# All of TensorE's products as pairs in its two row halves, with four equal PSUM tiles and written-out engine orders

## The chip, the core and the metric

The kernel runs on one core of a Trainium2 chip. The metric is device time in microseconds (us) of one execution. A core has five engines with instruction streams of their own: TensorE (PE in the profile, its weight loads PEld), VectorE (DVE), ScalarE (ACT), GpSimd (POOL) and SyncE (SP), which here issues DMAs. TensorE writes to PSUM, eight banks of 512 fp32 columns on 128 partitions.

## What is computed

Block-sparse attention over 4 batches, 8 heads, 768 tokens and 64 channels a head, followed by a feed-forward layer with a squared ReLU:

```python
scores = (q @ k.T) / 8                # per batch and head, 768 x 768
scores = where(mask, scores, -1e9)    # window, first and last block, 3 random blocks of 32
attn = exp(scores - max) / sum(...)
x = (attn @ v)                        # joined over heads: 3072 x 512
out = relu(x @ w_in)**2 @ w_out       # w_in 512 x 2048, w_out 2048 x 512
```

Inputs and output are fp32; the kernel multiplies in bf16.

## The kernel before

Heads are worked two at a time, as 16 units `u` (4 batches of 4 pairs). A head has 64 channels, so q and k of two heads fill the 128 partitions.

**Scores (L456, with L460 for a mask added as a product).** For 256 queries (128 at the start of batch 0) and two key blocks of 128, four matmuls with 64 rows each write one two-bank tile X: head 0 in TensorE's upper row half and bank 0, head 1 in the lower half and bank 1. ACT takes the exponential of the 1024 columns (L467) to the bf16 tile pT, DVE multiplies by the 0/1 mask MK (L474).

**Values (L496).** 128-row matmuls of 65 columns (64 channels and a column of ones for the sum) gather pT times V over six key blocks in the one-bank tile po. DVE normalizes (L504, L506) to xq; x is then transposed into xT, by TensorE in batch 0 (L513), by DMA later (L525).

**Feed-forward.** `hidden` (L554) multiplies w_in with xT into an X tile, for a unit of 768 columns (two blocks of 128 hidden rows for 384 queries) in batches 1 to 3, or 512 in batch 0, with 128 rows, four matmuls deep. `relu` goes to ACT (L563) or DVE (L565), `square` to POOL (L575) or ACT (L573), giving g. `output` (L598) sums 16 matmuls of 512 columns in the one-bank tile py for each 128 queries; it is copied to ys (L250 ACT, L252 DVE) and stored by SP (L607). For the last queries the output is cut into 512, 256, 128 and 128 columns, in py and X tiles by turns.

**PSUM.** X tiles of two banks (two at first, beside two single banks F for transposes and masks, later a third in the place of these), one bank po, one bank py.

**Order.** All instructions are tasks with assumed lengths. `run_schedule` walks through them at build time and picks what starts first, with keys, a pacing of the scores and small pseudo-random ties (`SEEDS`); the program is emitted in that order, so each engine's order is fixed at build. Scores are emitted in groups of one to three tiles (`GROUPS`), because a change between 64-row and 128-row matmuls has a price (`SWITCH`) there.

Of the kernel before, what the change touches and what calls it, by code (L numbers as in the profile page):

```python
# [19 lines left out]
P = 128  # L20
# [5 lines left out]
def kernel(  # L26
# [27 lines left out]
    TWM = 768  # L54
# [5 lines left out]
    PT_BUFS, R_BUFS, G_BUFS, XT_BUFS = 6, 4, 34, 3  # L60
# [4 lines left out]
    ps_o = ctx.enter_context(tc.psum_pool(name="ps_o", bufs=1))  # L65
    ps_y = ctx.enter_context(tc.psum_pool(name="ps_y", bufs=1))
# [8 lines left out]
    CB, GATES = 0.4, (6, 7)  # L75
    GROUPS = (1, 2, 2), (2, 2, 2), (2, 2, 3), (3, 3, 3)
    QT0, ADDED, ALONE = [(0, 128), (128, 128), (256, 256), (512, 256)], (0, 128), (0, 128)
# [4 lines left out]
    SWITCH, SHARE, SLACK = 0.096, 0.85, 0.1  # L82
    AHEAD = {"PE": 0.008, "DVE": 0.131, "ACT": 0.168, "POOL": 0.0, "SP": 0.0}
    LEAD = 6.401
    HOLD = 0
    PACE0, PACE, SINGLE, MASK_AT = 38.799, 1.711, 1, 17.0

    class Buf:
        def __init__(self, pool):
# [5 lines left out]
    TIES = 2.554, 0.816  # L99
    SEEDS = (  # L100
            512149, 706682, 47083, 521312, 863273, 189227, 137643, 472468, 522007,
            987534, 137643, 876738, 345072, 137643, 631945, 518011, 946966, 257531,
            137643, 137643, 206493, 528378, 381761, 582778)

    def tie(n):
        x = (n + 1) * 2654435761 & 0xFFFFFFFF ^ SEEDS[n // 64] * 2246822519 & 0xFFFFFFFF
        x = (x ^ x >> 15) * 2246822519 & 0xFFFFFFFF
        return (x ^ x >> 13) / 4294967296.0 - 0.5

    class Task:  # L110
        def __init__(self, engs, key, fn, deps=(), get=(), put=(), after=0.0, mode=None, dma=0.0, late=None, bias={}, port=False,
                     lead=0.0, yields=False, paced=False):
            self.engs = engs if isinstance(engs, dict) else dict([engs])
            self.key, self.fn = key, fn
            self.deps, self.get, self.put = list(deps), list(get), list(put)
            self.after, self.mode, self.dma, self.late, self.bias = after, mode, dma, late, bias
            self.port, self.lead, self.yields, self.paced = port, lead, yields, paced
            self.end = self.eng = None
            self.order = len(tasks)
            self.key += TIES[0 if key < 300 else 1] * tie(self.order)  # L120
            for b in self.put:
                b.holds += 1
            tasks.append(self)

    def run_schedule(free, bufs, dma_free, mode=128):
        taken = {name: [] for name in bufs}
        cells = [None] * 6
        paced = [t for t in tasks if t.paced]
        port = {"DVE": (0.0, 0.0), "POOL": (0.0, 0.0)}
        last = {"DVE": None, "POOL": None}  # L130
        waiting = list(tasks)
        ready = []
# [5 lines left out]
        singles = sum(b.pool == "X1" for t in tasks for b in t.get)  # L138

        def bank(pool, now):  # L140
            n, best = (1, None) if pool == "X1" else (2, None)
            for c in (4, 5) if pool == "X1" else (0, 2) if singles else (0, 2, 4):
                mine = [cells[i] for i in range(c, c + n)]
                if c in gone or any(b and b.holds for b in mine):
                    continue
                r = max([now] + [b.free for b in mine if b])
                k_ = (round(max([now] + [b.free + 0.8 for b in mine if b]), 4), c)
                if best is None or k_ < best[0]:
                    best = (k_, c, r)
            return best  # L150

        relaxed, gone = False, set()
        while waiting or ready:
            while paced and paced[0].end is not None:
                paced.pop(0)
            due = 1e9
            if paced and all(d.end is not None for d in paced[0].deps):
                due = max([paced[0].after] + [seen(d, "PE") for d in paced[0].deps])
            now = [t for t in waiting if all(d.end is not None for d in t.deps)]
            if now:  # L160
                gone = set(map(id, now))
                waiting = [t for t in waiting if id(t) not in gone]
                ready += now
            found, urgent = [], {}
            spare = sum(not any(b and b.holds for b in cells[c:c + 2]) for c in ((0, 2) if singles else (0, 2, 4)))
            for t in ready:
                r0 = t.after
                ok = True
                cnt, spot = {}, {}
                gone.clear()  # L170
                for b in t.get:
                    if b.pool in ("X1", "X2"):
                        x = bank(b.pool, free["PE"])
                        if x is None:
                            ok = False
                            break
                        gone.add(x[1])
                        spot[id(b)] = x[1]
                        r0 = max(r0, x[2])
                        continue  # L180
                    held = taken[b.pool]
                    at = len(held) + cnt.get(b.pool, 0) - bufs[b.pool]
                    cnt[b.pool] = cnt.get(b.pool, 0) + 1
                    if at >= 0:
                        if held[at].holds:
                            ok = False
                            break
                        r0 = max(r0, held[at].free)
                if not ok:
                    continue  # L190
                opt = None
                for e, us in t.engs.items():
                    r = max([r0, free[e]] + [seen(d, e) - t.lead for d in t.deps])
                    sw = SWITCH if e == "PE" and t.mode and t.mode != mode else 0.0
                    if e == "POOL" or (e == "DVE" and t.port):
                        p0, p1 = port["DVE" if e == "POOL" else "POOL"]
                        us += SHARE * max(0.0, min(r + us, p1) - max(r, p0))
                    if opt is None or r + us + t.bias.get(e, 0.0) < opt[3] - 1e-9:
                        opt = (r + us + sw, r, e, r + us + t.bias.get(e, 0.0))
                if t.yields and not relaxed and due - HOLD < opt[1] and spare <= len(paced[0].get):  # L200
                    continue
                found.append((round(opt[1], 4), t.key, t.order, t, opt, spot))
                if t.key < 100:
                    urgent[opt[2]] = min(urgent.get(opt[2], 1e9), opt[1])

            best = min((c for c in found if c[1] < 100 or c[0] + AHEAD[c[4][2]] < urgent.get(c[4][2], 1e9)),
                       key=lambda c: c[:3], default=None)
            if best is None and not relaxed:
                relaxed = True
                continue  # L210
            relaxed = False
            assert best is not None, "no task can start"
            t, (end, at, e, _) = best[3], best[4]
            t.eng = e
            t.end, free[e] = end, end - OVER[e]
            if e == "POOL" or (e == "DVE" and t.port):
                port[e] = (at, end)
                o = "DVE" if e == "POOL" else "POOL"
                more = SHARE * max(0.0, min(end, port[o][1]) - max(at, port[o][0]))
                if more and last[o]:  # L220
                    last[o].end += more
                    for b in last[o].put:
                        b.free = max(b.free, last[o].end + LAT[o])
                    free[o] += more
                    port[o] = (port[o][0], port[o][1] + more)
                last[e] = t
            if e == "PE" and t.mode:
                mode = t.mode
# [3 lines left out]
            for b in t.get:  # L232
                if b.pool in ("X1", "X2"):
                    b.at = best[5][id(b)]
                    cells[b.at] = b
                    singles -= b.pool == "X1"
                    if b.pool == "X2":
                        cells[b.at + 1] = b
# [5 lines left out]
            ready.remove(t)  # L244
            t.fn(e)
        return max(free.values())
# [54 lines left out]
    bm = consts.tile([nb, P], BF, name="bm")  # L301
# [4 lines left out]
    X = [ps_x.tile([P, 1024], F32, name=f"X{i}") for i in range(2)]  # L306
    first_pool = tc.psum_pool(name="ps_f", bufs=1)
    ps_f = first_pool.__enter__()
    FB = [ps_f.tile([P, 512], F32, name=f"F{i}") for i in range(2)]
# [527 lines left out]
```

## Time and profile before

| | |
|---|---|
| time, median of 3 runs | 271.95 us (270.59 to 272.35) |
| profiled execution, span | 270.3 us |
| TensorE busy | 260.7 us (96%), clock 1.0 from start to end |
| ACT / DVE / POOL busy | 220.8 / 174.4 / 93.4 us |
| matmul records, by row count | 2285 with 128 rows, 720 with 64, 2 with 24 (the program has 3048 matmuls) |
| HBM read, written | 27.3 MB, 6.3 MB |

A line of the groups reads: line, engine, operation, tiles, shapes, count, then busy us and mean ns of one, then the idle time just before and what ended it. "64*128" is a matmul in one row half; "128*128" takes the whole array. A TensorE row is longer than the matmul's share of the stream, because matmuls overlap in the array; the step from one start to the next is what a matmul costs in a run.

### The profile page before, as it was taken

How to read it: one execution, taken by the hardware profiler on the slowest of the kernel's cores; microseconds unless marked ns; L12 is line 12 of the kernel's file. 1: busy time of each engine (PE TensorE's matmuls, PEld its weight loads, DVE VectorE, ACT ScalarE, POOL GpSimd, SP SyncE). 2: the span in 40 equal slices, each digit the busy share in tenths (PEclk: the TensorE clock that was granted, in tenths of full speed). 3: DMA queues.
4: the chain of work that ended last, by engine and by line, in shares of the span. 5: the costliest groups of instructions: out<-in, count | busy, mean ns of one | idle time of the engine just before them, and what ended most of it. 6: DMA issues, size and time to landing. Idle time of an engine off the chain costs nothing.

```text
span 270.3 us, 7348 instructions
## 1 busy us (share of the span) xinstructions
PE 260.7 (96%) x3007; PEld 165.1 (61%) x3048; DVE 174.4 (65%) x337; ACT 220.8 (82%) x293; POOL 93.4 (35%) x114
## 2 busy tenths in 40 slices
PE   8999999999999999999999999999999999999993
PEld 5768866686665656555555555655665656555553
DVE  6788879988797999846886666777656654110100
ACT  3888999978999998999998789999989898455510
POOL 3290554746522045643343123122131123332300
PEclk9999999999999999999999999999999999999999
DMA  6999999999931238349951141336311102011022
GB/s 189 370 261 207 201 206 345 325 292 325 281 120 51 68 69 249 48 77 266 264 188 37 43 106 52 79 82 98 59 51 49 47 25 61 1 40 52 27 78 80
DMA packets 52026, 36.93 MB, mean 137 GB/s; under 512 B 31000, under 2 KB 49048, under 8 KB 51992
## 3 DMA queue, kind: packets, MB, share of 16 engines
q1 hardware_dynamic: 47224, 31.86, 43.2%
q0 software_dynamic: 4224, 4.19, 9.5%
q8 instruction: 24, 0.39, 0.6%
q10 hardware_dynamic: 544, 0.39, 0.5%
q14 instruction: 10, 0.08, 0.1%
HBM read 27.26 MB, written 6.29 MB: 124 GB/s over the span
## 4 chain that ended last, share of the span: by engine, by line
PE 85%; DMA 7%; DVE 5%; issue 2%; SPq 1%; ACT 1%; DVEq 0%; ACTq 0%
PE X L554 28%; PE py L598 26%; PE po L496 13%; PE X L456 13%; DVE pT L474 3%; DMA qs<-in_q_dram 3%; PE F L554 3%; DMA ks<-in_k_dram 2%; DMA out_dram<-ys 2%; PE X L598 1%; DVE xq L506 1%; PE F L378 1%; SPq L278 0%; PE F L408 0%; PE po L513 0%
## 5 line engine op out<-in xcount | busy, mean ns | idle before, releaser
L467 ACT ACTIVATE pT<-X 128x1024 bf16<-128x1024 f32 (+1 forms) x148 | 138.6, 1004 | 8.3 <-PE X L456 5.5
L474 DVE TENSOR_TENSOR pT<-pT,MK 128x1024 bf16<-128x1024 bf16 x132 | 103.0, 805 | 18.5 <-ACT pT L467 18.0
L575 POOL TENSOR_TENSOR g<-r 128x384 bf16<-128x384 f32 (+1 forms) x68 | 65.0, 961 | 130.2 <-ACT r L563 107.7
L598 PE MATMUL py<-w_out_sb,g 128*128 128x512 bf16 (+2 forms) x343 | 88.9, 367 | 3.0 <-issue 1.6
L554 PE MATMUL X<-xT,w_in_sb 128*128 128x384 bf16 (+1 forms) x512 | 90.8, 312 | 0.1
L554 PEld LDWEIGHTS <-w_in_sb 128*128 128x128 bf16 x640 | 54.4, 98 | 27.9 <-issue 1.0
L496 PEld LDWEIGHTS <-pT 128*128 128x128 bf16 x1152 | 47.3, 98 | 20.1 <-issue 6.2
L563 ACT ACTIVATE r<-X 128x768 f32<-128x768 f32 (+1 forms) x56 | 42.9, 766 | 19.0 <-PE X L554 17.4
L496 PE MATMUL po<-VT,pT 128*128 128x65 bf16 x1152 | 54.3, 194 | 0.6 <-DVE xq L506 0.2
L598 PEld LDWEIGHTS <-g 128*128 128x128 bf16 x416 | 34.7, 97 | 27.0 <-issue 3.8
L456 PE MATMUL X<-QK 64*128 64x256 bf16 (+1 forms) x624 | 46.1, 263 | 0.2
L456 PEld LDWEIGHTS <-QK 64*128 64x128 bf16 x624 | 25.4, 94 | 20.0 <-issue 16.1
L573 ACT ACTIVATE g<-r 128x384 bf16<-128x384 f32 (+1 forms) x52 | 27.9, 539 | 4.4 <-DVE r L565 3.0
L252 DVE COPY ys<-py 128x512 f32<-128x512 f32 (+1 forms) x14 | 9.2, 658 | 30.5 <-PE py L598 28.7
L252 POOL CAST VT<-vs 128x768 bf16<-128x768 f32 x15 | 15.4, 1024 | 30.1 <-issue 14.2
L504 DVE RECIPROCAL rs<-po 128x4 f32<-128x4 f32 (+1 forms) x52 | 9.2, 177 | 25.2 <-PE po L496 24.9
L506 DVE TENSOR_TENSOR xq<-po,rs 128x256 bf16<-128x256 f32 (+1 forms) x52 | 21.0, 404 | 1.8
L252 DVE CAST qc<-qs 128x768 bf16<-128x768 f32 (+2 forms) x16 | 9.1, 571 | 2.3 <-DMA qs<-in_q_dram 2.3
L250 ACT COPY ys<-py 128x512 f32<-128x512 f32 (+1 forms) x10 | 5.7, 571 | 5.5 <-PE py L598 5.3
L252 DVE CAST qc<-ks 128x768 bf16<-128x768 f32 (+1 forms) x13 | 9.8, 759 | 0.1
L565 DVE TENSOR_SCALAR r<-X 128x512 f32<-128x512 f32 (+1 forms) x8 | 6.6, 824 | 3.3 <-PE X L554 2.7
L554 PE MATMUL F<-xT,w_in_sb 128*128 128x128 bf16 x128 | 8.3, 219 | 0.0
(59 smaller groups left out, 90.4 us busy)
## 6 DMA issues: line engine op xcount, KB each, us to landing
vs<-in_v_dram SPq DMA_DIRECT2D x16, 384.0 KB, 6.2
out_dram<-ys SPq DMA_DIRECT2D x23, 256.0 KB, 2.2
ks<-in_k_dram SPq DMA_DIRECT2D x15, 384.0 KB, 5.3
qs<-in_q_dram SPq DMA_DIRECT2D x12, 384.0 KB, 4.8
w_in_sb<-in_moe_w_in_dram POOLq DMA_DIRECT2D x4, 512.0 KB, 9.5
w_out_sb<-in_moe_w_out_dram POOLq DMA_DIRECT2D x4, 512.0 KB, 16.3
qs<-in_q_dram SPq DMA_DIRECT2D x4, 256.0 KB, 8.2
xT<-xq SPq DMA_TRANSPOSE x36, 2.3
```

The source lines that it names most:

```text
L252: (V if e == "DVE" else G).tensor_copy(out=out, in_=in_)
L456: nc.tensor.matmul(ps[:, h, j * w:(j + 1) * w], QK[i][hs, 1, ksl], QK[i][hs, 0, qsl], start=j == 0, stop=not add, skip_group_check=True)
L467: A.activation(out=pT[:, :, 0:n], in_=stile.pop(a)[:, :, 0:n], func=AF.Exp, scale=scale)
L474: V.tensor_tensor(out=pT, in0=pT, in1=m[:, None].broadcast_to([P, 2, len(cs), w]), op=AOP.mult)
L496: nc.tensor.matmul(po[:, qc, h, :], pT[:, h, j * w + qc * P:j * w + (qc + 1) * P], VT[i][:, h, n, 0:VW], start=(n == 0 and qc == 0 and h = ...
L504: V.reciprocal(out=rs, in_=po[:, :, :, D:VW])
L506: V.tensor_tensor(out=xq, in0=po[:, :, :, 0:D], in1=rs.broadcast_to([P, n, 2, D]), op=AOP.mult)
L554: nc.tensor.matmul(htile[T, f][:, i], w_in_sb[:, kc, (f + i) * P:(f + i + 1) * P], xT[b][:, kc, c0:c0 + w], start=(kc == 0), stop=(kc == K ...
L563: A.activation(out=to, in_=src, func=AF.Relu)
L573: A.activation(out=g, in_=r, func=AF.Square)
L575: (G if e == "POOL" else V).tensor_mul(out=g, in0=r, in1=r)
L598: nc.tensor.matmul(ytile[T, i], gtile[T, f][:, ts * P:(ts + 1) * P], w_out_sb[:, f, cs[0]:cs[1]], start=(f == 0), stop=(f == NF - 1))
```

## The change

Every product is now made of 64-row matmuls, issued in pairs by `pair`: one in the upper half, one in the lower, into the two banks of one tile. Where the contraction has 128 rows (values, hidden, output), the work goes over its list twice: in the first pass half 0 writes bank 0 and half 1 bank 1, in the second pass ("crossed") half 0 adds to bank 1 and half 1 to bank 0. The two banks hold different results: two heads, two sets of hidden rows, two blocks of 128 queries or two ranges of columns. Between the passes `change_places` makes TensorE wait for the last matmul of the first pass, by a semaphore of its own; in the built program this wait stands on the next weight load.

PSUM is four two-bank tiles X for everything. Hidden units have 1024 columns; all tiles of batches 1 to 3 have 256 queries; an output accumulation covers 256 queries (two banks of 512). Values start only when all three pT tiles of their queries are there. Scores are no longer grouped. Buffers: 8 pT (6 before), 3 r (4), 13 g of 1024 columns (34 of 512). `run_schedule` with its keys, pacing and ties is replaced by `run_orders`, which takes each engine's task order from a list in the file (`ORDERS`), and so also fixes which of ACT, DVE and POOL does a task. The matmul count goes from 3048 to 5932.

```diff
+    HALVES = slice(0, D), slice(D, P)
+    def pair(out, lhsT, rhs, crossed=False, **kw):
+        for r, rows in enumerate(HALVES):
+            last = nc.tensor.matmul(out(r ^ crossed), lhsT(r ^ crossed, rows), rhs(r ^ crossed, rows), skip_group_check=True, **kw)
+        return last.ins
+
+    def change_places(last):
+        tc.add_manual_dep(nc.tensor.nop().ins, last.name, SYNC, reason="the other row half writes the bank next")
...
     def values(...):
-                    nc.tensor.matmul(po[:, qc, h, :], pT[:, h, j * w + qc * P:j * w + (qc + 1) * P], VT[i][:, h, n, 0:VW],
-                                     start=(n == 0 and qc == 0 and h == 0), stop=n == NCH - 1,
-                                     skip_group_check=True)
+                    last = pair(lambda h: po[:, h, qc], lambda h, rows: pT[rows, h, j * w + qc * P:j * w + (qc + 1) * P],
+                                lambda h, rows: VT[i][rows, h, n, 0:VW], crossed, start=not crossed and n == 0 and qc == 0,
+                                stop=crossed and n == NCH - 1)
...
     def hidden(T, f, part, parts, buf, e):
-            nc.tensor.matmul(htile[T, f][:, i], w_in_sb[:, kc, (f + i) * P:(f + i + 1) * P], xT[b][:, kc, c0:c0 + w],
-                             start=(kc == 0), stop=(kc == KM - 1))
+        crossed = part >= parts // 2
+        if part == parts // 2:
+            change_places(hlast.pop((T, f)))
+        work_ = [(j, kc) for j in range(n) for kc in range(KM)]
+        k_ = len(work_) * 2 // parts
+        for j, kc in work_[part % (parts // 2) * k_:(part % (parts // 2) + 1) * k_]:
+            hlast[T, f] = pair(lambda i: htile[T, f][:, i, j * w:(j + 1) * w],
+                               lambda i, rows: w_in_sb[rows, kc, (f + i * n + j) * P:(f + i * n + j + 1) * P],
+                               lambda i, rows: xT[b][rows, kc, c0:c0 + w], crossed,
+                               start=not crossed and kc == 0 and j == 0, stop=crossed and kc == KM - 1)
...
     def output(...):
-            nc.tensor.matmul(ytile[T, i], gtile[T, f][:, ts * P:(ts + 1) * P], w_out_sb[:, f, cs[0]:cs[1]],
-                             start=(f == 0), stop=(f == NF - 1))
+            ylast[T, i] = pair(lambda c: ytile[T, i][:, c], lambda c, rows: gtile[T, f][rows, tokens(c)],
+                               lambda c, rows: w_out_sb[rows, f, columns(c)], crossed,
+                               start=not crossed and f == 0, stop=crossed and f == NF - 1)
...
-    run_schedule({"PE": 4.4, "DVE": 4.4, "ACT": 3.65, "POOL": 3.7, "SP": 16.0},
-                 {"po": 1, "y": 1, "pT": PT_BUFS, "r": R_BUFS, "g": G_BUFS, "ys": YS_BUFS,
+    run_orders(ORDERS, {"PE": 4.4, "DVE": 4.4, "ACT": 3.65, "POOL": 3.7, "SP": 16.0},
+                 {"y": 1, "S": 2, "H": 2, "po": 2, "pT": PT_BUFS, "r": R_BUFS, "g": G_BUFS, "ys": YS_BUFS,
```

The transposes by TensorE and the mask products are turned into pairs in the same way, and 14 idle matmuls that keep TensorE busy in the opening stay.

## The prediction

> **What bounds the kernel now.** I read the busy shares and the chain first, then the groups, then TensorE's timeline at single groups.
>
> ```profile
> PE 260.7 (96%) x3007; PEld 165.1 (61%) x3048; DVE 174.4 (65%) x337; ACT 220.8 (82%) x293; POOL 93.4 (35%) x114
> PEclk9999999999999999999999999999999999999999
> PE 85%; DMA 7%; DVE 5%; issue 2%; SPq 1%; ACT 1%; DVEq 0%; ACTq 0%
> ```
>
> TensorE is busy for 96% of the span at full clock and is 85% of the chain; DMA is on the chain only in the opening (until 16.6 us) and in the last store. So the question is what TensorE's time consists of. A matmul's row is longer than its share of the stream, so I use the distance from start to start.
>
> ```profile
> 240.65 1.14 PE L554 MATMUL X<-xT,w_in_sb 128*128 128x384 bf16 x6
> 241.63 0.59 PE L598 MATMUL py<-w_out_sb,g 128*128 128x512 bf16 x2
> 242.06 1.14 PE L554 MATMUL X<-xT,w_in_sb 128*128 128x384 bf16 x6
> ...
> 149.63 1.46 PE L598 MATMUL py<-w_out_sb,g 128*128 128x512 bf16 x6
> 151.02 0.83 PE L456 MATMUL X<-QK 64*128 64x256 bf16 x12
> 151.78 0.66 PE L496 MATMUL po<-VT,pT 128*128 128x65 bf16 x16
> 152.27 0.38 PE L598 MATMUL py<-w_out_sb,g 128*128 128x512 bf16 x1
> ```
>
> Columns: start, length, engine and line, operation, count. Six matmuls of 384 columns take 0.98 us (163 ns each), two of 512 take 0.43 (216), sixteen of 65 take 0.49 (30.2 ns over the whole trace). The second block has the switches. The six 512s need 1.30 us but the scores start 1.39 after them; the scores are six pairs in the two row halves (64*128), 110 ns a pair inside the run, 0.66 in all, but what follows starts 0.76 after them. Each change between 128 rows and 64 rows costs about 0.1 us. Over the whole trace the first matmul after a change ends 106 ns later than the same matmul without one, in both directions.
>
> ```profile
> 7.04 0.23 PE L456 MATMUL X<-QK 64*128 64x128 bf16 x2
> 7.10 0.22 PE L460 MATMUL X<-R,oh 64*128 64x128 bf16 x2
> 7.16 0.22 PE L456 MATMUL X<-QK 64*128 64x128 bf16 x2
> ...
> 7.05 0.10 PEld L460 LDWEIGHTS <-oh 64*128 64x128 bf16 x2
> 7.11 0.10 PEld L456 LDWEIGHTS <-QK 64*128 64x128 bf16 x2
> ```
>
> Two matmuls of 64 rows, one in each half, take 56 ns together for 128 columns; singly a 128-row one takes 55.8. Within a pair both weight loads and both matmuls start 3 to 4 ns apart.
>
> The account of before: values 1152 x 30.2 ns = 34.8 us; scores 264 pairs x 109.3 + 96 pairs x 55.8 = 34.3; hidden 384 x 163 + 128 x 109.3 + 128 x 55.8 = 83.7; output 368 x 216 + 16 x 109.3 + 32 x 55.8 = 83.0; transposes, masks and warm-up 8.6. That is 244.4 us of stream (by the program's counts; 41 matmul records are missing in the trace). TensorE's instruction list changes its row count 147 times: 147 x 106 ns = 15.6 us. Of the 270.3 us, 10.3 remain: 4.3 lost in the first 10 us, 4.2 after TensorE's last row at 266.07, 1.8 anywhere else. There is almost no wait left to remove; the switches are the only reserve.
>
> **The change, part by part.**
> *Switches:* every matmul is now a 64-row one, so all 147 go: -15.6 us. In the first 16.6 us, where the chain runs through the loads of k and q, 19 of them (2.0 us) may be worth nothing; I count them as lost.
>
> *Stream:* the counts are from the built program. Hidden: 704 pairs of 256 columns x 110 + 128 pairs of 128 x 56 = 84.6 us. Output: 320 pairs of 512 x 217 (the single's 216 and the 1 ns that pairs cost more elsewhere) + 96 x 110 + 32 x 56 + 64 pairs of 64 columns x 31 = 83.8. Scores 34.4. Transposes in pairs of 64 columns 2.2, masks 1.3, warm-up 2.3. Values: 1152 pairs of 65 columns, a size that no row shows in pairs. From below, the single's 30.2 ns (34.8 us); from above, the 128-column pair's 56 (64.5 us), or two singles in a row, 60.4 (69.6 us). I take 32, near the lower end, because pairs of 128 and 256 columns cost only 0 to 1 ns over a single: 36.9 us. Sum 245.5 us, 1.1 more than now.
>
> [...]
>
> *The turn:* a half may write the other's bank only when the last matmul of the first pass is complete (change_places), so a weight load waits for TensorE's own semaphore, 115 times, and all of TensorE's later work stands behind it. A matmul's row outlasts its stream by 0.16 us (a 256-column pair: 269 against 110), and an engine starts 0.04 to 0.09 after what it waits for: about 0.3 us, between 0.1 (a switch's drain) and 0.35. What hides it is work put between the passes: I priced the instructions between each first pass and its turn. Nearly all after 24 us have 0.38 us or more (a score tile of 0.44, four hidden pairs of 0.44, a pass of values of 0.38). Before the end the deficit is 1.8 us; without any cover it would be 115 x 0.3 = 35.
>
> *The end:* the last output now goes in four accumulations into one tile, X0, with nothing between. Four turns, 1.2 us; three copies, each 0.2 us to start, 0.58, 0.29 and 0.37 long, 0.09 back to TensorE: 2.1. Now the end looks like this:
>
> ```profile
> 265.01 1.06 PE L598 MATMUL py<-w_out_sb,g 128*128 128x128 bf16 x16
> 265.27 0.29 DVE L252 COPY ys<-X 128x128 f32<-128x128 f32 x1 [8.91 <-PE X L598]
> 267.36 0.29 DVE L252 COPY ys<-py 128x128 f32<-128x128 f32 x1 [1.80 <-DMA out_dram<-ys]
> ```
>
> The last copy waits for an older store to free its buffer. With the accumulations spread over the copies that store will be done, so 2.9 us follow the last matmul instead of 4.2.
>
> *The other engines:* relu goes largely to DVE (29 of 48 units), squares to ACT.
>
> ```profile
> L467 ACT ACTIVATE pT<-X 128x1024 bf16<-128x1024 f32 x132 | 126.2, 1025 | 6.7 <-PE X L456 5.5 <-PE po L496 0.4
> L563 ACT ACTIVATE r<-X 128x768 f32<-128x768 f32 x44 | 35.7, 811 | 17.8 <-PE X L554 16.4 <-POOL g L575 0.4
> L565 DVE TENSOR_SCALAR r<-X 128x768 f32<-128x768 f32 x4 | 3.8, 956 | 0.7 <-PE X L554 0.7
> ```
>
> By lengths stretched from these rows (ACT 1.02 and DVE 1.22 us for a relu of 1024 columns, ACT 1.06 for a square), ACT stays at about 221 us, DVE rises from 174 to about 194, POOL falls from 93 to about 66. All remain under TensorE's 245, so I cost this at nothing; TensorE's stream covers it. SP issues fewer stores of the same bytes, and its order of loads and transposes gets new waits, but those were never last after 16.6 us: nothing, 0 to 2 us.
>
> *Four tiles:* scores, hidden, output and values share four two-bank tiles, instead of three (two in the opening) plus one bank each for po and y. I add no wait for it and price it among the rivals.
>
> *Sum:* 245.5 + 4.3 (opening) + 2.0 (lost there) + 1.8 (idle as now) + 1.8 (turns) + 3.3 (end) + 2.9 (after it) = 261.6 us of span. The runs' median of 271.95 is 1.65 above the profiled 270.3, so 263.3 us.
>
> **The rivals.**
> *Small pairs cost more (slower than before).* Place: the 104 passes of values. Mechanism: 48 instructions in a pass, four every 30 ns, more than the two halves or the queue take. Each ns over 32 costs 1.15 us; the saving of 8.7 us is gone from 39.5 ns a pair. At 45 ns it is 278 us, at 56 ns 291. For it: the fastest sustained stretch in the trace is 13 to 14 ns an instruction (the 128-column pairs), this needs 7.5. Against: the pairs there are bound by their columns, and when a queue has filled behind a switch, six instructions start within 18 ns. [...]
> *Tiles come free late.* 264 times a tile is taken. By the rows a score tile is held 1.75 us, a hidden unit about 4, values 2.3, an output some 15: near 740 of 4 x 258 tile-us, 72%. If each taking were 30 ns late on the average, the saving would be gone: 267 to 277 us. For it: the order on TensorE is a fixed list, so one late relu holds everything. Against: the order now is fixed at build too, and only 1.8 us are idle.
> *The halves do not overlap at all in the crossed pass or with 512 columns:* the hidden and output work doubles, +84 us or more, 350 us. Only L456 and L460 show pairs, but nothing sets them apart.
>
> **How the numbers follow.** Forecast as summed 0.66 (its own range 258 to 267); late tiles 0.18; small pairs 0.13; no overlap 0.03. About 1% (269.2 to 274.7) is what a measurement of this kernel can tell from no change. Faster: 0.66 and 0.08 of the late tiles, 0.74. Same: 0.06 of the late tiles and 0.01 of the small pairs, 0.07. Slower: the rest, 0.19. The range 257 to 279 leaves out about 0.05 below and 0.11 above.
>
> **What would show it.** Right: no form but 64*128 on TensorE; 110 ns for a 256-column pair, 217 for 512, 30 to 34 for 65; idle ahead of turns under 4 us before the end; first matmul to last some 256 us. Wrong: 65-column pairs at 40 ns or more; "issue" or relu and copy named as what TensorE's loads wait for, over 8 us in sum; a switch cost that stays under another name at each turn.

## The result, and the profile after

The changed kernel takes 281.08 us (median of 4 runs, 280.24 to 282.18) against 271.94 us for the kernel before: a ratio of 1.0343 (95% interval 1.03 to 1.0387). It is slower by 3.4%; 263.3 had been forecast. The profiled execution has a span of 278.5 us (280.24 with what lies around it).

The page of the changed kernel; the digits are tenths of busy time and of the granted clock in 40 slices of 7 us:

```profile
PE 256.3 (92%) x5932; PEld 205.9 (74%) x5932; DVE 182.9 (66%) x342; ACT 208.4 (75%) x230; POOL 56.9 (20%) x69
PE   7697757999998999899999999999999999999974
PEclk9978999999999999999999999999999999999999
q8 instruction: 46, 0.75, 1.2%
PE 71%; DVE 8%; DMA 8%; issue 5%; SPq 3%; ACT 3%; DVEq 0%; ACTq 0%
```

From the eighth slice on the kernel is near what had been forecast. The loss is in the first seven slices, in which TensorE is idle for a quarter of the time and the clock drops. "issue", time in which an engine waited for nothing that the profile shows, was 2% of the chain and is 5%. The kernel before had 24 packets in q8 and none of the clock's dips.

The same in stretches of 10 us (PE, PEld, DVE, ACT, POOL busy with counts, clock, DMA share, GB/s), first the changed kernel, then the one before:

```profile
20.00:30.00 10.00, 8.11 (x235) 6.48 (x230) 6.26 (x20) 7.55 (x10) 3.24 (x5) 0.83 1.22 199
30.00:40.00 10.00, 6.83 (x250) 6.10 (x245) 6.81 (x15) 6.64 (x8) 0.00 (x0) 1.00 1.17 220
50.00:60.00 10.00, 10.00 (x257) 9.00 (x253) 6.56 (x12) 8.39 (x12) 0.00 (x0) 1.00 0.03 7
```

```profile
30.00:40.00 10.00, 9.80 (x155) 6.95 (x155) 7.67 (x13) 9.74 (x17) 5.82 (x5) 1.00 1.08 199
```

From 30 to 40 us the DMA engines are full in both kernels (share 1.17 and 1.08), and all engines of the changed one are idle for a third of the time, so none of them holds the others up by its own work. TensorE's waits in the first 50 us, with the time in all, the count and the longest, are mostly not for data either:

```profile
PE X L241 <- issue: 7.5, 5, 2.1
PE X L335 <- issue: 1.2, 1, 1.2
PE X L241 <- DVE bm L230: 1.2, 1, 1.2
PE X L241 <- DVE QK L180: 1.1, 2, 0.6
```

On TensorE's timeline these stops lie inside runs of alike matmuls:

```profile
34.42 0.83 PE L241 MATMUL X<-xT,w_in_sb 64*128 64x128 bf16 x23
37.31 0.44 PE L241 MATMUL X<-xT,w_in_sb 64*128 64x128 bf16 x9 [2.06 <-issue]
...
40.15 0.46 PE L241 MATMUL X<-xT,w_in_sb 64*128 64x128 bf16 x10
42.13 0.32 PE L241 MATMUL X<-xT,w_in_sb 64*128 64x128 bf16 x5 [1.52 <-issue]
...
45.85 0.38 PE L241 MATMUL X<-w_out_sb,g 64*128 64x256 bf16 x3
47.78 0.48 PE L241 MATMUL X<-w_out_sb,g 64*128 64x256 bf16 x5 [1.56 <-issue]
```

A pass of 32 hidden matmuls stops after the 23rd. The 24th reads the same tiles as those before it. Counted in TensorE's own list (weight loads and matmuls, from the trace's records), the stops stand 256 instructions apart, and q8's packets have 16 KB. So each packet is 256 instructions of 64 bytes, and the stops stand on the packets' borders. For each border, from the records (us; the stop is what the step to the first instruction has over its price):

```
border  packet before entered  packet starts   ends   first instruction   stop
 1              7.97               11.36      12.47        13.90          1.45
 2             13.90               16.01      17.09        19.26          0
 3             19.26               22.91      23.85        25.20          1.39
 4             25.20               28.93      29.91        31.39          1.20
 5             31.39               35.08      36.05        37.32          2.22
 6             37.32               39.67      40.64        42.14          1.68
 7             42.14               45.29      46.21        47.79          1.71
 ...
31            182.46              182.38     183.32       187.56          0
32            187.56              187.41     188.62       192.56          0
```

At borders 31 and 32, where the DMA engines are quiet (a share of 0.01 from 182 to 187 us), the packet starts 0.08 and 0.15 us ahead of TensorE's entry into the packet before. In the opening it starts 2 to 4 us after. It takes 0.9 to 1.1 us there, and the instruction that waits for it runs 1.3 to 1.6 us after its end: 4.8 to 6.2 us in all. TensorE now uses up 256 instructions in 3.3 to 5.1 us there (from the entry to the end of the last row before the stop). The one other stop of this kind (0.97 us, at 86.5 us) also stands on a border, the 14th, whose packet starts 3.95 us after the entry at a DMA share over 1. The seven sum to 10.6 us.

### The profile page after: what moved, and what is told of

The parts are those of the page before. It is cut to its first block, busy times and chain, and to the rows that moved or that the text cites. A ratio compares the mean times of both kernels' runs of the same rounds, so it can differ in the third digit from the quotient of the medians.

```text
span 278.5 us, 12982 instructions
## 1 busy us (share of the span) xinstructions
PE 256.3 (92%) x5932; PEld 205.9 (74%) x5932; DVE 182.9 (66%) x342; ACT 208.4 (75%) x230; POOL 56.9 (20%) x69
## 4 chain that ended last, share of the span: by engine, by line
PE 71%; DVE 8%; DMA 8%; issue 5%; SPq 3%; ACT 3%; DVEq 0%; ACTq 0%
PE X L241 70%; DVE pT L397 4%; DMA QK<-qc 2%; DMA vs<-in_v_dram 2%; SPq L449 2%; DMA xT<-xq 2%; ACT pT L390 2%; DMA out_dram<-ys 1%; DVE r L494 1%; SPq L206 1%; DVE xq L426 1%; PE X L335 1%; ACT ys L178 1%; DVE ys L180 0%; DVE rs L424 0%
## 5 line engine op out<-in xcount | busy, mean ns | idle before, releaser
L241 PE MATMUL X<-xT,w_in_sb 64*128 64x256 bf16 (+1 forms) x1664 | 103.2, 261 | 5.4 <-issue 4.6
L241 PE MATMUL X<-w_out_sb,g 64*128 64x512 bf16 (+3 forms) x1024 | 99.0, 323 | 3.8 <-issue 1.6
L241 PEld LDWEIGHTS <-w_in_sb 64*128 64x128 bf16 x1664 | 79.5, 94 | 13.2 <-issue 6.9
L241 PEld LDWEIGHTS <-g 64*128 64x128 bf16 x1024 | 45.9, 94 | 27.2 <-issue 4.3
L505 POOL TENSOR_TENSOR g<-r 128x512 bf16<-128x512 f32 (+1 forms) x17 | 25.5, 1508 | 155.1 <-ACT r L492 134.5
L241 PE MATMUL X<-VT,pT 64*128 64x65 bf16 x2304 | 54.5, 192 | 2.7 <-DVE pT L397 1.4
L241 PEld LDWEIGHTS <-pT 64*128 64x128 bf16 x2304 | 50.6, 95 | 8.1 <-DVE pT L397 1.8
L494 DVE TENSOR_SCALAR r<-X 128x1024 f32<-128x1024 f32 x29 | 35.3, 1221 | 20.4 <-PE X L241 20.2
L503 ACT ACTIVATE g<-r 128x1024 bf16<-128x1024 f32 (+1 forms) x43 | 38.5, 906 | 9.4 <-DVE r L494 9.2
L426 DVE TENSOR_TENSOR xq<-X,rs 128x256 bf16<-128x256 f32 (+1 forms) x52 | 21.0, 404 | 2.0 <-DVE rs L424 0.3
L180 POOL CAST VT<-vs 128x768 bf16<-128x768 f32 x11 | 10.1, 920 | 12.4 <-DMA vs<-in_v_dram 8.4
L241 PE MATMUL X<-R,oh 64*128 64x128 bf16 (+1 forms) x114 | 10.6, 242 | 0.0
```

Source lines behind the costliest of these rows:

```text
L180: (V if e == "DVE" else G).tensor_copy(out=out, in_=in_)
L241: last = nc.tensor.matmul(out(r ^ crossed), lhsT(r ^ crossed, rows), rhs(r ^ crossed, rows), skip_group_check=True, **kw)
L426: V.tensor_tensor(out=xq.rearrange("p c h d -> p h c d"), in0=po[:, :, :, 0:D], in1=rs.broadcast_to([P, 2, n, D]), op=AOP.mult)
L494: V.tensor_scalar(out=to, in0=src, scalar1=0.0, scalar2=None, op0=AOP.max)
L503: A.activation(out=g, in_=r, func=AF.Square)
L505: (G if e == "POOL" else V).tensor_mul(out=g, in0=r, in1=r)
```

## The experiments

The theory, called theory 1 or the theory of the instruction packets: the doubled matmul count makes TensorE use up its packets faster than the opening's full DMA queues deliver them. Each kernel ran beside the kernel before (271.5 to 272.0 us).

**1. Fewer instructions in the opening.** In the changed kernel, batch 0's values and its hidden work of 128 queries go back to one 128-row matmul per bank: 416 matmuls fewer, and 68 changes between 64 and 128 rows back (an estimated 68 x 106 ns = 7.2 us).

```diff
@@ values
+        whole = u < HP
+                    if whole:
+                        h = int(crossed)
+                        nc.tensor.matmul(po[:, h, qc], pT[:, h, ...], VT[i][:, h, n, 0:VW], ...)
+                        continue
@@ hidden: the same, where the width is 128
```

> The changed kernel with 128-row matmuls, one per bank and pass, for batch 0's values and for its two hidden tiles of 128 queries: 416 fewer matmuls and 832 fewer TensorE instructions in the opening, but 68 switches of row count (68 x 0.106 = 7.2 us). Theory 1 (instruction fetch): TensorE stops in the opening because its instructions come in packets of 256 that are requested when the packet before is entered and come late while the DMA engines are busy; with fewer instructions a packet lasts longer, so the six stops of 1.3 to 2.3 us at packet borders before 48 us shrink to under 4 us in sum and the half-clock stretches go: 270 to 277 us despite the switches. Theory 2 (order and tiles): the opening waits for data that come late in the fixed order; then the switches come on top: 281 to 288 us, stops where they were.

Measured: 273.35 us (10 runs), 1.0067 [1.0037, 1.0096] of the kernel before. TensorE's waits up to 50 us, where "issue" is gone:

```profile
PE X L241 <- DVE warm L227: 1.2, 1, 1.2
PE X L241 <- DVE QK L180: 0.4, 1, 0.4
PE X L443 <- DVE xq L432: 0.3, 2, 0.2
```

Its packets still start 1 to 3.5 us after the entry, but the first instruction comes 1.5 us after the packet's end at the first border, just in time, and 2.4 to 4.3 us after it at the next ones: no border stop before 50 us (one of 0.5 us stands at 81 us), and the clock stays up (0.996 against 0.986). 416 of 5932 matmuls, 7%, decide, and the kernel pays some 7 us of switches and still gains.

**2. The hidden part alone**, 128 rows in two tiles only (28 changes).

```diff
-        whole = u < HP
+        whole = False
```

> The changed kernel with 128-row matmuls only in the two hidden tiles of 128 queries (128 fewer matmuls, all between 29 and 47 us; 28 switches, 3.0 us). Theory 1: the stops at 12 and 24 us, ahead of these products, stay at 1.3 to 1.7 us; those at 30, 35, 40 and 46 us shrink to a half or less in sum: span 275 to 279 us. Theory 2 (data and order): all six stay, +3 us of switches.

Measured: 277.14 us (one run). The stops at 12.4 and 24.0 us, ahead of the hidden work, stay (1.5 us each); the four from 30 to 46 us shrink to one of 0.7 at 36.9 us and one of 0.3 at 48.0.

**3. Only the count.** Experiment 1 with its 128-column hidden matmuls cut in two of 64 columns: no pairs, no turns, the same columns.

```diff
-                nc.tensor.matmul(htile[T, f][:, i, j * w:(j + 1) * w], ...
+                for z in range(2):
+                    z0, z1 = z * w // 2, (z + 1) * w // 2
+                    nc.tensor.matmul(htile[T, f][:, i, j * w + z0:j * w + z1], ...
```

> The first experiment's kernel with each of its 128 hidden matmuls of 128 columns cut into two of 64 columns: as many TensorE instructions there as with pairs, but no pair, no second pass and no wait for TensorE itself; stream about 0.8 us more. Theory 1 (what counts is the number of instructions): a packet lasts about 5 us again between 27 and 48 us, and with a fetch 2 to 3.7 us late stops of 0.3 to 1.5 us stand at packet borders again: 1 to 4 us more than the 271.8 of that run. Rival (the stops come of the two passes or their waits): no stop at a border, at most 1 us more.

Measured: 276.88 us (one run), 3.5 over experiment 1, where 1 to 4 had been expected. Its waits up to 50 us begin with

```profile
PE X L491 <- issue: 2.9, 3, 1.4
```

L491 is the cut matmul. The two long ones stand on borders, 30.97 to 32.48 and 37.10 to 38.67 us, and so does the short one, of 0.2 us at 25.7. So neither the pairs nor the turns are needed for them.

**4. The old kernel with more instructions.** Before, with batch 0's hidden and output matmuls and its 256-column scores cut in halves by columns: 448 matmuls more, nothing else.

```diff
+            k_ = 2 if b == 0 else 1
+            for z in range(k_):
+                z0, z1 = z * w // k_, (z + 1) * w // k_
+                nc.tensor.matmul(htile[T, f][:, i, z0:z1], ...
```

> The kernel before with batch 0's hidden, output and 256-column score matmuls cut into two of half the columns: 448 more matmuls and 896 more TensorE instructions before 75 us, 128-row as they were, no other order; by the rows 1.6 us more of stream. Theory 1: packets last about 5.3 us instead of 7 between 20 and 50 us while the DMA engines are busy, so stops of 0.5 to 1.5 us come at three to five packet borders: 273.5 to 277 us of span. Theory 2: only the stream, 272 us.

Measured: 274.87 us (one run; 271.64 for the kernel before beside it). The old kernel gets the same kind of stop, three times (0.8, 1.8 and 0.9 us idle, at 27, 33 and 39 us). The first two on its timeline:

```profile
25.70 0.54 PE L559 MATMUL F<-xT,w_in_sb 128*128 128x64 bf16 x13
27.03 1.65 PE L559 MATMUL F<-xT,w_in_sb 128*128 128x64 bf16 x51 [0.79 <-issue]
...
29.42 1.71 PE L559 MATMUL F<-xT,w_in_sb 128*128 128x64 bf16 x53
32.95 0.48 PE L559 MATMUL F<-xT,w_in_sb 128*128 128x64 bf16 x11 [1.82 <-issue]
```

From the first stop to the second there are 51 + 16 + 8 + 53 = 128 matmuls (16 and 8 in the lines left out), each with its weight load: 256 instructions. The third stop comes 256 instructions after the second. So more instructions alone bring the stops, in a kernel with none of the change's other parts.

**5. Less DMA.** The changed kernel without w_out's loads; its output products read w_in's tile.

```diff
-            G.dma_start(out=w_out_sb[:, ns, :], in_=wov[:, ns, :])
+            pass
```

> The changed kernel without its four loads of w_out (2 MB); the output products read w_in's tile in their place, so the result is another, the work on TensorE the same. Theory 1: from about 28 us on the DMA engines are free sooner, instruction packets start under 1 us after their request, and the stops at 35, 40 and 46 us (2.3, 1.7 and 1.8 us) go or fall under 0.5 us each; the stops at 12 and 24 us stay: 5 to 7 us less, some 273 to 276 us. Theory 2: TensorE's products and tiles are the same, so the time stays within 2 us of the changed kernel's.

Measured: 281.65 us (one run), a miss. The loads of later q, k and v wait for those of the weights, so they moved into the gap and the DMA engines stayed nearly full: a share of 0.91 and 310 GB/s from 30 to 40 us instead of 1.17 and 220. One packet starts 4.6 us after the entry, and the stop there grows:

```profile
33.85 0.83 PE L241 MATMUL X<-xT,w_in_sb 64*128 64x128 bf16 x23
38.10 0.69 PE L241 MATMUL X<-xT,w_in_sb 64*128 64x128 bf16 x9 [3.42 <-issue]
```

The stops at 30 and 46 us are gone, that at 40 shrinks to 0.3, and those at 12 and 24 us stay. In the first 50 us the stops sum to 7.0 us instead of 9.7, but the time did not fall: after 50 us TensorE loses some 2.5 us more than in the changed kernel, among it a wait of 2.4 us for a mask and two new stops on borders (0.6 us at 107, 1.0 at 134). Which transfers hold the packets up does not follow from this run.

**6. and 7. More DMA later.** Nine loads of 384 KB by POOL, into old buffers, added to the changed kernel at about 186 us and to the one before at about 157.

```diff
+        if u == NU - 1:
+            for i in range(9):
+                old = raw[12 + i // 3][i % 3]
+                G.dma_start(out=old.rearrange("p t n d -> p t (n d)"), in_=(qv, kv, vv)[i % 3][3, i // 3])
```

> The changed kernel with nine more loads of 384 KB, which nothing reads, issued by POOL at about 186 us, where the DMA engines are quiet and TensorE has no stop. Theory 1: for some 12 us the packets of instructions start 2 to 4 us late, a packet lasts 5 us there, so one to three new stops of 0.5 to 2 us appear, each at a packet border (instruction 195 of 256 by the program's count): 1 to 4 us more. Theory 2: TensorE stops only for data, so no new stop stands at a border; at most a wait for transposed x.

> The kernel before with the same nine loads, issued by POOL at about 157 us. Theory 1: a packet of 256 instructions lasts 11 us there, longer than any lateness seen, so no stop at a border: within 1 us of before. Theory 2 says the same of the borders; if the loads themselves hurt, through data or POOL's squares, it shows here as in the run on the changed kernel.

Measured: 290.99 and 278.34 us (one run each). Neither shows a stop on a border where the loads were added. In the first, TensorE waits 7.4 us for a transposed x; in the second, 5.1 us for a mask behind a late k. In the first a packet does start 4.7 us after the entry (0.8 without the loads), but TensorE was waiting for data anyway. So added loads make a packet late here too; that it stops TensorE at this place is not shown. The opening of the first kernel is the changed kernel's, and it repeats: stops on six borders before 50 us, 10.0 us in sum.

**8. The end.** Experiment 1, with the last four accumulations in four tiles instead of one.

```diff
-            ytile[T, i] = tile_of(buf)[:, :, 0:w]
+            ytile[T, i] = (X[(0, 3, 1, 2)[i]] if T == TILES[-1] else tile_of(buf))[:, :, 0:w]
```

> The first experiment's kernel with the last four output accumulations in four different PSUM tiles in place of one. The three waits for the copy (0.83, 0.60 and 0.62 us over the turn) go, the turns of 0.23 us stay: 2 us less, about 271.3 us, level with the kernel before (270.5 to 272).

Measured: 271.19 us (10 runs), 0.998 [0.9954, 1.0006]: level with the kernel before, 2.2 us below experiment 1. The three copies no longer stand in TensorE's way.

**9. POOL beside DVE.** Experiment 8, with two of POOL's squares given to ACT.

```diff
     "ACT":  ... 395, 402, 934, 405, 408, 415,
+    "ACT":  ... 395, 402, 940, 934, 405, 408, 946, 415,
-    "POOL": ... 940, 946, 472, ...
+    "POOL": ... 472, ...
```

> The kernel of the fewer early matmuls with the end in four tiles, and two of POOL's squares (1024 columns, 2.1 us each) given to ACT at the same place of the order. Theory (POOL and DVE slow each other): the two masks of 4.47 us at 103 us, beside POOL's squares, fall to about 0.69 us each, so DVE reaches the reciprocal that follows some 2 to 3 us earlier, and TensorE's idle time of 100 to 120 us (about 4 us) falls by as much: 268.3 to 269.5 us, below the kernel before by about 1%. Rival (the idle time there comes from the order on TensorE and ACT, and DVE's long masks are only beside it): the masks may get short, ACT has 2.1 us more to do in the same place, and the time is 271 us or more.

Measured: 271.58 us (12 runs), 0.9977 [0.9948, 1.0005]. DVE's two masks at that place, first in experiment 8, then here:

```profile
103.05 4.47 DVE L397 TENSOR_TENSOR pT<-pT,MK 128x1024 bf16<-128x1024 bf16 x2 [0.24 <-ACT pT L390]
```

```profile
104.04 2.14 DVE L397 TENSOR_TENSOR pT<-pT,MK 128x1024 bf16<-128x1024 bf16 x2 [1.61 <-ACT pT L390]
```

The masks went from 2.2 and 2.4 us to 0.9 and 1.3 (0.68 elsewhere; POOL's casts still lie beside them). But they start 1 us later, since ACT is late now, and TensorE's wait of 2.4 us for the mask became two for ACT, 1.1 and 0.6. Half of the theory holds; the time came out as the rival had it.

**10. and 11. The turns at the end.** Experiment 9, with each first pass of the last four accumulations put between the passes of the one before it; then the same with two buffers of their own for the 128-column results. (For the new order two output accumulations may be open at once, one before.)

```diff
-    1233, ..., 1240, 1253, ..., 1260, 1243, ..., 1250, 1263, ..., 1270
+    1233, ..., 1236, 1253, ..., 1256, 1237, ..., 1240, 1243, ..., 1246, 1257, ..., 1260,
+    1263, ..., 1266, 1247, ..., 1250, 1267, ..., 1270
@@ out_copy, in the second kernel only
+        else:
+            ys = work.tile([P, P], F32, name="ysl", tag="ysl", bufs=2)
```

> The kernel with POOL's two squares on ACT, and in the last four output accumulations each first pass now stands between the first and second pass of the one before it. Theory (a turn costs 0.23 us only where nothing stands between the passes): four turns of 0.23 us go, about 0.7 to 0.9 us less than the kernel it is made from, near 268 us. Rival (the 0.23 us is the cost of changing the banks, wherever it stands): no change to that kernel, within 0.2 us.

> The kernel with the mixed passes at the end, and the two output copies of 128 columns write staging buffers of their own instead of the ring of three. In the profile of the kernel it is made from, TensorE's last matmul ends at 263.3 us and the last copy starts at 265.91, after an older store has freed its buffer. Theory (the 0.96 us that the mixed passes saved, and 1.4 us of the moved squares, ended in that wait): the last copy follows the last matmul in 0.1 us, 2.4 us less in the span: 269.0 to 269.8 us, about 1% below the kernel before. Rival (the stores themselves stand in a row, and the last one ends when it did): the copy comes earlier and the last store lands as late as now, 271.4 us or more.

Measured: 271.64 us (12 runs), 0.9982 [0.9958, 1.0006], and 270.39 us (12 runs), 0.9969 [0.9945, 0.9993]. The last run of output matmuls in experiment 9 took 6.97 us; in experiment 10 it takes 6.01, and the last copy waits:

```profile
257.29 6.01 PE L241 MATMUL X<-w_out_sb,g 64*128 64x256 bf16 x232 [0.32 <-ACT g L515]
...
265.91 0.29 DVE L180 COPY ys<-X 128x128 f32<-128x128 f32 x1 [4.05 <-DMA out_dram<-ys]
```

The 0.96 us of four turns are saved in that run of matmuls as expected, and the last copy then waits for an older store that holds the staging buffer. With buffers of their own:

```profile
258.49 6.01 PE L241 MATMUL X<-w_out_sb,g 64*128 64x256 bf16 x232 [0.32 <-ACT g L515]
...
264.55 0.29 DVE L180 COPY ysl<-X 128x128 f32<-128x128 f32 x1 [1.47 <-PE X L241]
```

The copy follows at once. The span fell by 0.8 us (269.1 to 268.3), not 2.4: in this execution the same run of matmuls began 1.2 us later, and from the last copy's start to the end of the span it took 3.8 us instead of 3.2, so part of the rival holds too. This kernel is the fastest of all. It lies 0.3% below the one before; the interval just leaves 1 out, but this is less than the 1% that the prediction took as what can be told from no change.

## Why the prediction was wrong

*What held.* A pair of 256 columns costs 109 ns. For pairs of 65 columns here are two passes of values between other matmuls:

```profile
177.82 0.53 PE L241 MATMUL X<-VT,pT 64*128 64x65 bf16 x24
178.18 0.60 PE L241 MATMUL X<-QK 64*128 64x256 bf16 x8
178.62 0.53 PE L241 MATMUL X<-VT,pT 64*128 64x65 bf16 x24
178.99 1.03 PE L241 MATMUL X<-w_out_sb,g 64*128 64x512 bf16 x8
```

Twelve pairs take 0.37 us from start to start, 30.7 ns a pair, which is also the median of all passes (32 taken). The mean after 50 us is 33, because a few passes hold a wait, such as the stop at 86.5 us. So the rival of the small pairs, 45 ns or more, did not come, nor did that of halves that do not overlap. Matmuls follow at 15.3 ns on the average here, 30.7 within one half. No form but 64*128 and no switch is left. From 50 to 260 us TensorE does 9.7 of every 10 us at these prices, least from 100 to 120 us (8.6). ACT and POOL are at 208 and 57 us (221 and 66 forecast), DVE at 183 (194). First matmul to last takes 274.0 us, where some 256 had been named.

*The turns and the end.* Here is TensorE's chain at the end (start, length, what):

```profile
270.11 0.66 PE X L241 x32
...
270.85 0.30 DVE ys L180
271.15 0.04 issue
271.19 1.08 PE X L241 x32
272.27 0.05 issue
272.32 1.09 PE X L241 x32
273.41 0.02 issue
273.43 0.38 ACT ys L178
```

From 271.19 to 272.32 lie 16 pairs of 56 ns, 0.90 us: the turn costs 0.23 (0.3 taken). The three copies cost 0.83, 0.60 and 0.62 us, 2.05 in all (2.1 taken). The span ends 3.3 us after the last matmul's row (2.9 taken).

*What failed.* The step is *Stream*, and the *Sum* that rests on it: 5932 matmuls in the place of 3048 were priced by their columns alone, at full clock, and the opening was carried over from before (4.3 + 2.0). No term stands for what brings TensorE its instructions; *The other engines* asks only whether ACT, DVE, POOL and SP keep up, and these did. The sum was 261.6 us; the span is 278.5, 16.9 more:
- 10.6 us are the seven stops on packet borders. Experiments 1, 3 and 4 show the cause: taking 416 matmuls out removes the six in the opening, cutting columns puts stops back, and the old kernel gets them too.
- About 3.2 us are half clock. The granted clock is 0.5 from 14.92 to 18.33 and from 25.16 to 28.57 us, behind the stops at 12.4 and 24.0; the matmuls started in these windows are worth 1.6 us each time at full clock, and some 0.5 of the second was a wait for data. The windows are 3.41 us long. With neither stop, in experiment 1, both windows are at 1.00. Which stop tips the clock is not shown: in experiments 5 and 6 the half-clock windows before 50 us begin at 27.4 and 27.6 us, and at 37.7 and 37.8.
- The other 3.1 us are a balance. At the prices measured, the stream is 242.4 us, 3.1 less than the 245.5 of the sum. Against it stand some 6 us of waits beyond those allowed for, about 4 in the first 50 us. The longest after that are a DVE mask at 114 us (1.2), transposed x at 253 us (0.6 in two waits) and two waits of 0.3 us for a PSUM tile, at 102 and 110 us. So the rival of late tiles was real and small.

No rival named the cause. The page before held its row, q8 with 24 packets. By the counts in its stretches of 10 us (410, 403 and 310 instructions from 10 to 40 us) TensorE took 6.2 to 8.3 us for 256 of them, just longer than the 4.8 to 6.2 that a packet needs in the full opening; this kernel cuts the one to 3.3 to 5.1 and not the other. The forecast of under 4 us ahead of turns did hold: two turns before the end stand fully open, at 0.24 and 0.23 us, and the four at the end. The sign that showed the loss is "issue" with no turn in front of it.

Against the kernel before, the exchange stands so. By 50 us the changed kernel has done 27.1 us of its stream and the one before 38.6: 11.5 lost. From there to the end it takes 13.1 beside what is left of its stream (278.5 - 50 - 215.3), the one before 14.5 (270.3 - 50 - 205.8): 1.4 gained. With a stream that is 2.0 shorter (242.4 against 244.4), that is the 8.2 us between the spans within 0.1. So past the opening, too, the change brings only some 3 us, where 8.7 in all had been forecast: waits, the turns and copies at the end among them, took the place of most of the switches.

## What to carry to other kernels

A matmul split into a pair costs next to nothing in the array here (30.7 ns against 30.2 for 65 columns) and still costs two instructions more, a matmul and a weight load, and these came by DMA like the data: their packets started 2 to 4 us after the entry where the DMA engines were full (a share of 1.17 from 30 to 40 us). So where TensorE's count rises, divide 256 by its instructions per us, stretch by stretch, and hold that against the time that an instruction packet needs in that stretch (the start behind the entry, its length, and what follows it); where DMA is full, keep the large matmuls, and split only where it is quiet. "issue" in the middle of a run of alike instructions, at equal distances in the engine's count (256 here), was the mark of it.

## What the runs showed of the hardware

- TensorE's instructions came in packets of 16 KB, 256 at a time, one packet ahead: the next started -0.9 to 1.3 us from the entry into the one before where the DMA share was under 0.5 (206 packets of the changed kernel and nine of its variants), and 0.5 to 4.9 us after it where the share was 1 or over (144 packets, median 2.4); the waiting instruction ran 1.3 to 1.6 us after the packet's end in the changed kernel.
- In the changed kernel 3.41 us at half clock came twice (from 14.92 and from 25.16 us), behind stops of 1.4 to 1.5 us and the waits beside them; stops of up to 2.2 us from 30 us on brought none there, but in experiment 6 a half-clock window began during the one of 2.2 us at 36 to 38.
- Two row halves took 65-column matmuls at 15.3 ns each on the average (30.7 ns a pair) in the changed kernel. A change of rows cost 106 ns in the kernel before, a wait of TensorE for its own last matmul 230 ns in the changed one, where no work stands between.
- DVE's masks of 1024 columns took 0.68 us, and 2.2 and 2.4 us while POOL squared 1024 columns (experiment 8); with POOL's casts beside them, 0.9 and 1.3 (experiment 9).
